# A fused attention and expert layer: sharing the first pooling, splitting stage 1 in 256 and 320 columns, and five smaller moves

## The chip, the core and the metric

The kernel runs on one core of a Trainium2 chip. A core has five engines with a queue of instructions each: TensorE (PE, matmuls; its weight loads are shown as PEld), VectorE (DVE), ScalarE (ACT), GpSimd (POOL) and SyncE (SP, which only issues transfers here). They run side by side and wait for each other through semaphores. The metric is the device time of one execution in microseconds (us).

## What is computed

Attention over keys and values that are averaged in groups of eight, and then a layer of eight experts with a fixed capacity. Cut to what matters:

```python
# q, k, v: 8 batches, 8 heads, 576 positions, 64 per head
k_p, v_p = mean of k, v over groups of 8 positions      # 72 left
scores = q @ k_p^T / 8 ; attn = softmax(scores) ; x = attn @ v_p
x = x as 4608 tokens of 512
logits = x @ w_gate                                     # 4608 x 8
order = argsort(-logits.flatten())
for idx in order:                                       # greedy
    tok, e = idx // 8, idx % 8
    if tok is free and expert e has under 576 tokens: assign tok to e
out[mask_e] = relu(x[mask_e] @ w1[e]) @ w2[e]           # 512 -> 1024 -> 512
```

All is float32. The greedy assignment fills one expert after another; the kernel finds, expert by expert, the threshold at which an expert is full, and the experts are computed in the order in which they fill.

## The kernel before

**Attention.** The 4608 tokens are 36 tiles of 128; a batch is four and a half tiles. For tile n the loop records: `st_s(n)`, scores of q against the pooled keys `kblk` into the PSUM tile `pss` (one buffer, so the next scores wait until softmax has read it); `st_e(n-1)`, transposes of the exponentials; `st_av(n-2)`, the product with `vblk` into `psa`; `softmax(n)`, a maximum (L181) and a subtraction (L182) on DVE and the exponential (L183) on ACT; and `norm(n-3)` on DVE, after which ACT's queue stores tile x to DRAM (`xd`). One instruction stream per engine is recorded in that order, and each engine works its stream strictly in order.

Ahead of a batch its k is pooled by `pool_k` (sums of halves, L117, L118, L121, the last writes `kblk`) and its v by `pool_v` (L133 to L135 write the sums `vsum`; then `vblk` gets its blocks, L139 by six ACT activations for the first v or L142 as one masked product). `prep_v` and `prep_g` are the small transposes and gate products that complete `vblk` (L150 to L161). The first k and v are pooled by DVE, all later ones by POOL, at tiles that the table `at` names with `plan`. The loads are issued by SP in the order k, q, v; those of the first batch are cut into halves. `warm(n)` records n matmuls of ones by ones whose result nobody reads; 16 of them stand ahead of the first tile, six after each of tiles 0 and 1.

**Search.** `Routing` works on logits of 128 x 36 x 8. `bounds` finds their largest and smallest value, in three steps that `A.run` places after given norms of the attention's last third. Then, per expert, some rounds of comparing (DVE L520) and counting (PE L525) narrow the threshold. `close` turns the selection into a list of rows (`rows`, `halves`), counts which expert got how much (`per`, `pc`, then PE L671 `rt<-pc,ones` and DVE's `left`), checks the result (`bad`) and takes the chosen tokens out of the logits with two masks (L695, L696). It is a generator; each `yield` names how long the next piece needs, and a piece is called a step.

**Experts.** The rows of x are gathered by POOL (`xg`, five tiles of up to 128 rows), transposed by PE (L916) into `tp`, and split into a rounded part `xh` (ACT L918) and the rest `xl` (DVE L920). Weights are split likewise: `w1h` (ACT L892), `w1l` (DVE L896). Stage 1 (L936) makes h = xh·w1h + xh·w1l + xl·w1h, for two column halves of 288 tokens and eight groups of 128 hidden units each; ACT and DVE split the relu of it into `hh` and `hl`. Stage 2 (L963, 512 columns, four token tiles, and L974 for the remaining 64 tokens) multiplies with w2, ACT copies and POOL scatters rows to the output.

The order of all this is written by a planner in `experts`: `now` counts estimated PE time along the matmuls of stages 1 and 2, `dve` estimated DVE time, and pieces of the next expert's search, its weight splits (`Pieces`) and its transposes (`turn`) are recorded between matmuls when their estimated time has come; `later` holds back DVE work. For the first expert there is no stage before it, so its steps are written out one after the other.

**End.** After the experts `suspect` makes a flag from `bad` (PE L750, DVE L751). All engines load the flag (L1011), and a branch runs `experts_one_by_one` if it is set.

Of the kernel before, what the change touches and what calls it, by code (L numbers as in the profile page):

```python
# [21 lines left out]
class Attention:  # L22
# [100 lines left out]
    def pool_v(self, b, eng, halves=(slice(0, 6),), first=False):  # L123

        src = self.rv[b]
        t1 = self.wk.tile([96, 6, 256], F32, name="t1", bufs=1)
        t2 = self.wk.tile([96, 6, 128], F32, name="t2", bufs=1)
        if b not in self.sums:
            self.sums[b] = self.wk.tile([96, 6, 64], F32, name="vsum")
        s = self.sums[b]  # L130
        for c in halves:
            n = c.stop - c.start
            eng.tensor_tensor(t1[:, c], src[:, c, :256], src[:, c, 256:], op=OP.add)  # L133
            eng.tensor_tensor(t2[:, c], t1[:, c, :128], t1[:, c, 128:], op=OP.add)
            eng.tensor_tensor(s[:, c], t2[:, c, :64], t2[:, c, 64:], op=OP.add)  # L135
            if first:
                for m in range(c.start, c.stop):
                    for i in range(2):
                        self.nc.scalar.activation(self.vblk[b % 4][:96, m, i, :64], s[:, m], AF.Copy,  # L139
                                                  scale=self.mask[:, m, i:i + 1])  # L140
            else:
                eng.tensor_tensor(self.vblk[b % 4][:96, c, :, :64], s[:, c, None, :].to_broadcast([96, n, 2, 64]),  # L142
                                  self.mask[:, c, :, None].to_broadcast([96, n, 2, 64]), op=OP.mult)
# [94 lines left out]
    def finish(self, after):  # L238

        i, j = self.nt - 2, self.nt - 1  # L240
        rinv = {}
        self.st_e(j, 0)
        self.st_av(i, 0)
# [19 lines left out]
    def run(self, ctx, consts, after, end, warm):  # L263
# [22 lines left out]
        for b in (1, 2):  # L286
            self.load_k(b)
            self.load_v(b)
            self.load_q(b)
# [11 lines left out]
        for n in range(nt):  # L301
# [5 lines left out]
            if n == 2:  # L307
                self.prep_v(0)
                self.prep_g(0)
# [7 lines left out]
            if n < 2:  # L317
                self.pool_v(0, nc.vector, vh[n:n + 1], n == 0)
# [16 lines left out]
class Routing:  # L335
# [76 lines left out]
    def warm(self, n):  # L412


        ps = self.psum()
        for _ in range(n):
            self.nc.tensor.matmul(ps, self.ones, self.ones[:, None].to_broadcast([128, 4, 128]), start=True, stop=True)  # L417
# [327 lines left out]
    def suspect(self, flag):  # L745
        nc = self.nc
        b = self.wk.tile([128, 1], BF, name="rc")
# [3 lines left out]
        nc.vector.tensor_scalar(flag, ps[:1, :1], 0.0, None, op0=OP.is_gt)  # L751

# [86 lines left out]
class Experts:  # L839
# [82 lines left out]
    def stage1(self, later=lambda after, t, f: f()):  # L922
# [5 lines left out]
        for u in range(2):  # L928
            for f in range(8):
                o = slice(288 * u, 288 * u + 288)  # L930
                ps = self.psA.tile([128, 512], F32, name="h", bufs=5)
                n = 0
                for a, b in ((self.w1h, self.xh), (self.w1l, self.xh), (self.w1h, self.xl)):
                    for j in range(4):
                        fs = slice(128 * f, 128 * f + 128)
                        nc.tensor.matmul(ps[:, :288], a[:, j, fs], b[:, j, o], start=(n == 0), stop=(n == 11))  # L936
                        n += 1
                        if n < 12:
                            yield 0.133
                yield 0.133  # L940
                nc.scalar.activation(hh[:, f, o], ps[:, :288], AF.Relu)  # L941
                if u:
                    nc.scalar.activation(hr[:, f], ps[:, 224:288], AF.Relu)
                later(0.65, 0.4, lambda f=f, o=o, ps=ps: nc.vector.scalar_tensor_tensor(  # L944
                    hl[:, f, o], ps[:, :288], 0.0, hh[:, f, o].bitcast(F32), op0=OP.max, op1=OP.subtract))
# [39 lines left out]
def kernel(ctx, tc, q, k, v, wblk, moe_w1, moe_w2, out):  # L985
# [15 lines left out]
    with ExitStack() as c2:  # L1001
# [3 lines left out]
        A.run(c2, lambda: R.consts(A.jp, A.ident), {NC - 13: [step], NC - 12: [step], NC - 11: [step], NC - 5: [lambda: R.best(0, NC - 4)]},  # L1005
              R.begin(g), R.warm)
    with ExitStack() as c2:
        experts(c2, tc, g, R, xd, moe_w1, moe_w2, out, A.ident, cap)
    flag = cst.tile([1, 1], I32, name="flag")
    R.suspect(flag)  # L1010
    flag = nc.values_load(flag[0:1, 0:1], min_val=0, max_val=1)  # L1011
# [5 lines left out]
def experts(ctx, tc, g, R, xd, w1, w2, out, ident, cap):  # L1017

# [10 lines left out]
    now, dve, ready = 0.0, 0.0, 0.0  # L1029
# [12 lines left out]
    def step(e):  # L1042

        nonlocal now, ready, dve
# [17 lines left out]
        since[p, what] = now  # L1062

# [60 lines left out]
    eids = {}  # L1124
    while (0, "rows") not in since:
        step(0)

# [18 lines left out]
    last = 0.0  # L1146
    for e in range(8):
# [27 lines left out]
        if more:  # L1175
# [5 lines left out]
            for t in range(turned[e + 1], 3):  # L1181
                turn(e + 1, t)
        flush(2)
    flush()

# [74 lines left out]
```

## Time and profile before

| | us |
|---|---|
| median of 3 runs | 653.32 |
| lowest and highest | 651.98, 653.77 |
| profiled execution, its own time | 653.45 |
| its span | 651.7 |
| PE busy in the span | 610.7 (94%) |
| DVE busy | 399.7 (61%) |
| ACT busy | 241.3 (37%) |
| POOL busy | 187.5 (29%) |
| mean granted PE clock | 0.967 of full speed |

The span is measured from the first instruction to the last; 1.75 us of the profiled execution lie around it. The stages follow each other in time: attention to about 151, search and the way into the first expert to about 187, experts to 637, then the end. A row of the timeline has the start, the duration, the engine, the line, what is written and read, and in brackets how long the engine had been idle and what ended that. The row of a window has the busy time and the number of instructions of each engine. Busy time of PE includes time in which a matmul runs at half the clock.

### The profile page before, as it was taken

How to read it: one execution, taken by the hardware profiler on the slowest of the kernel's cores; microseconds unless marked ns; L12 is line 12 of the kernel's file. 1: busy time of each engine (PE TensorE's matmuls, PEld its weight loads, DVE VectorE, ACT ScalarE, POOL GpSimd, SP SyncE). 2: the span in 40 equal slices, each digit the busy share in tenths (PEclk: the TensorE clock that was granted, in tenths of full speed). 3: DMA queues.
4: the chain of work that ended last, by engine and by line, in shares of the span. 5: the costliest groups of instructions: out<-in, count | busy, mean ns of one | idle time of the engine just before them, and what ended most of it. 6: DMA issues, size and time to landing. Idle time of an engine off the chain costs nothing.

```text
span 651.7 us, 12033 instructions
## 1 busy us (share of the span) xinstructions
PE 610.7 (94%) x4638; PEld 528.2 (81%) x4638; DVE 399.7 (61%) x1137; ACT 241.3 (37%) x550; POOL 187.5 (29%) x203
## 2 busy tenths in 40 slices
PE   6899999996689999999999999999999999999990
PEld 3799999885389769877987997898799889879970
DVE  8677777878668577857874686387458327406200
ACT  3344444442335134514433353243336325415210
POOL 5899999000300330313301301130120112020010
PEclk9799999997779999999999999999999999999996
DMA  9999994111450524504501910460181055013011
GB/s 306 300 361 320 336 335 177 65 66 66 138 194 2 188 93 139 189 33 160 213 17 39 319 32 34 154 219 10 41 310 46 32 180 193 16 57 131 1 48 30
DMA packets 32291, 91.10 MB, mean 140 GB/s; under 512 B 3456, under 2 KB 3456, under 8 KB 29760
## 3 DMA queue, kind: packets, MB, share of 16 engines
q1 hardware_dynamic: 21008, 61.87, 27.8%
q0 software_dynamic: 5888, 18.88, 8.4%
q10 hardware_dynamic: 5328, 9.49, 4.3%
q8 instruction: 38, 0.62, 0.4%
q14 instruction: 29, 0.24, 0.1%
HBM read 71.35 MB, written 18.87 MB: 138 GB/s over the span
## 4 chain that ended last, share of the span: by engine, by line
PE 73%; issue 13%; DVE 8%; POOL 2%; ACT 1%; POOLq 0%; DVEq 0%; ACTq 0%
PE h L936 26%; PE h L963 20%; PE psa L206 8%; PE pss L171 5%; PE h L974 3%; PE tp L916 2%; PE pse L196 2%; PE rt L196 2%; POOL out_dram L950 1%; PE rt L645 1%; PE rt L562 1%; DVE e L182 1%; POOL xg L884 1%; PE rt L417 1%; PE rt L160 1%
## 5 line engine op out<-in xcount | busy, mean ns | idle before, releaser
L950 POOL DMA_INDIRECT out_dram<-yt,rows x32 | 33.9, 1061 | 289.8 <-ACT yt L967 289.5
L963 PE MATMUL h<-w2l,hh 128*128 128x512 f32 x256 | 102.2, 399 | 0.0
L963 PE MATMUL h<-w2h,hl 128*128 128x512 f32 x256 | 102.1, 399 | 0.0
L963 PE MATMUL h<-w2h,hh 128*128 128x512 f32 x256 | 101.2, 395 | 0.0
L936 PE MATMUL h<-xl,w1h 128*128 128x288 f32 x512 | 93.3, 300 | 3.6 <-DVE xl L920 3.6
L936 PE MATMUL h<-xh,w1l 128*128 128x288 f32 x512 | 95.2, 301 | 0.4 <-DVE late L1131 0.2
L936 PE MATMUL h<-xh,w1h 128*128 128x288 f32 x512 | 92.7, 300 | 0.7 <-ACT xh L918 0.7
L941 ACT ACTIVATE hh<-h 128x288 fp32r<-128x288 f32 x128 | 52.7, 412 | 100.7 <-PE h L936 95.6
L936 PEld LDWEIGHTS h<-xl,w1h 128*128 128x128 f32 x512 | 76.6, 189 | 3.8 <-DVE xl L920 3.8
L936 PEld LDWEIGHTS h<-xh,w1h 128*128 128x128 f32 x512 | 75.7, 189 | 4.3 <-issue 2.7
L936 PEld LDWEIGHTS h<-xh,w1l 128*128 128x128 f32 x512 | 76.6, 189 | 1.8 <-DVE w1l L896 0.8
L944 DVE SCALAR_TENSOR_TENSOR hl<-h,hh 128x288 fp32r<-128x288 f32 x128 | 57.5, 452 | 32.9 <-ACT hh L941 19.6
L206 PE MATMUL psa<-vblk,eT 97*128 97x146 f32 (+1 forms) x480 | 67.9, 294 | 0.5 <-DVE vblk L161 0.4
L884 POOL DMA_INDIRECT xg<-xd,rows x40 | 39.5, 988 | 94.5 <-DVE rows L656 60.4
L967 ACT ACTIVATE yt<-h 128x512 f32<-128x512 f32 x32 | 19.1, 598 | 122.7 <-PE h L963 106.2
L206 PEld LDWEIGHTS psa<-vblk,eT 97*128 97x128 f32 (+1 forms) x480 | 58.3, 183 | 2.5 <-issue 2.0
L963 PEld LDWEIGHTS h<-w2h,hl 128*128 128x128 f32 x256 | 48.2, 188 | 8.6
L963 PEld LDWEIGHTS h<-w2h,hh 128*128 128x128 f32 x256 | 48.2, 188 | 8.6
L963 PEld LDWEIGHTS h<-w2l,hh 128*128 128x128 f32 x256 | 48.3, 189 | 8.3
L171 PE MATMUL pss<-kblk,rawq 128*128 128x144 f32 (+1 forms) x320 | 44.1, 296 | 3.3 <-POOL eT L80 1.6
L896 DVE TENSOR_TENSOR w1l<-raw,w1h 128x512 fp32r<-128x512 f32 x64 | 41.0, 684 | 9.7 <-ACT w1h L892 9.5
L905 DVE TENSOR_TENSOR w2l<-raw,w2h 128x512 fp32r<-128x512 f32 x64 | 43.3, 683 | 0.5
(195 smaller groups left out, 907.8 us busy)
## 6 DMA issues: line engine op xcount, KB each, us to landing
raw<-in_moe_w_dram SPq DMA_DIRECT2D x64, 512.0 KB, 5.9
xd<-xt ACTq DMA_DIRECT2D x36, 256.0 KB, 6.3
rawk<-in_k_dram SPq DMA_DIRECT2D x7, 1152.0 KB, 13.5
rawv<-in_v_dram SPq DMA_DIRECT2D x7, 1152.0 KB, 16.5
rawq<-in_q_dram SPq DMA_DIRECT2D x7, 1152.0 KB, 12.1
rawk<-in_k_dram SPq DMA_DIRECT2D x2, 576.0 KB, 4.0
rawv<-in_v_dram SPq DMA_DIRECT2D x2, 576.0 KB, 9.7
rawq<-in_q_dram SPq DMA_DIRECT2D x1, 640.0 KB, 10.7
```

The source lines that it names most:

```text
L171: nc.tensor.matmul(ps[cols, j // 2, 144 * (j % 2):144 * (j % 2) + 144], self.q_of(b, j, n, cols.stop - cols.start), self.kblk[b % 4][:, j] ...
L196: nc.tensor.transpose(ps[:96, 128 * m:128 * m + 128], self.e[i][:, 96 * c:96 * c + 96], self.ident)
L206: self.nc.tensor.matmul(o[h], self.eT[i][:, g, 128 * m + h.start:128 * m + h.stop], self.vblk[b % 4][:, 3 * g + m], start=(m == 0), stop=( ...
L884: nc.gpsimd.indirect_dma_start(out=self.xg[:n, t, :], out_offset=None, in_=self.xd, in_offset=bass.IndirectOffsetOnAxis(ap=rows[:n, t:t + ...
L896: self.nc.vector.tensor_tensor(l, raw, h.bitcast(F32), op=OP.subtract)
L905: self.nc.vector.tensor_tensor(self.w2l[:, i], self.raw2[e][:, i], self.w2h[:, i].bitcast(F32), op=OP.subtract)
L936: nc.tensor.matmul(ps[:, :288], a[:, j, fs], b[:, j, o], start=(n == 0), stop=(n == 11))
L941: nc.scalar.activation(hh[:, f, o], ps[:, :288], AF.Relu)
L944: later(0.65, 0.4, lambda f=f, o=o, ps=ps: nc.vector.scalar_tensor_tensor(hl[:, f, o], ps[:, :288], 0.0, hh[:, f, o].bitcast(F32), op0=OP. ...
L950: st = nc.gpsimd.indirect_dma_start(out=rows, out_offset=bass.IndirectOffsetOnAxis(ap=idx, axis=0), in_=y, in_offset=None)
L963: nc.tensor.matmul(ps, a[:, f, o], b[:, f], start=(f == 0 and k == 0), stop=(f == 7 and k == 2))
L974: nc.tensor.matmul(ps[64 * a:64 * a + 64, :256], self.hr[:, f], self.raw2[e][:, f, 256 * a:256 * a + 256], start=(f == 0), stop=(f == 7))
```

## The change

- The first half of the first v is pooled by POOL, the second half by DVE, which now comes after the second tile's softmax. The buffers t1 and t2 are made once per batch, so both halves share them.
- The second k is pooled by DVE instead of POOL, in two halves, after the softmax of tile 2. Of the second q the part that the first tiles need is loaded ahead of the second v, the rest behind it. Four more idle matmuls stand ahead of `prep_v(0)`.
- The order of the last `st_e` and `st_av` in `finish` is swapped in one place.
- The three steps of `bounds` come two tiles later.
- In the search of the first expert three idle matmuls follow a step of the search that is announced with 1.25 or 2.2, and eight one with 2.6. They write to a tile `h` of the experts' PSUM.
- For the first expert the counts of `pc` come ahead of the ten idle matmuls, the first four weight splits ahead of `left` and the checks, and two tiles instead of three are transposed before stage 1 begins.
- Stage 1 goes over columns 0 to 255 and then 256 to 575, instead of two halves of 288; before stage 1 of every later expert two tiles are turned.
- The flag is made at the 24th matmul of the last stage 2 and loaded at the 48th.

```diff
+        self.pool_v(0, nc.gpsimd, vh[:1], True)
         for b in range(1, B):
-            plan(first[b - 2] + 1 if b > 2 else b, self.pool_k, b, nc.gpsimd)
+            if b == 1:
+                plan(2, self.pool_k, b, nc.vector, kh)
+            else:
+                plan(first[b - 2] + 1 if b > 2 else b, self.pool_k, b, nc.gpsimd)
...
+        n = 4 * self.cut(1)
+        self.load_k(1)
+        self.load_q(1, slice(0, n))
+        self.load_v(1)
+        self.load_q(1, slice(n, 4 * S))
...
             if n == 2:
+                warm(4)
                 self.prep_v(0)
...
-            if n < 2:
-                self.pool_v(0, nc.vector, vh[n:n + 1], n == 0)
+            if n == 1:
+                self.pool_v(0, nc.vector, vh[1:])
...
         i, j = self.nt - 2, self.nt - 1
-        self.st_e(j, 0)
         self.st_av(i, 0)
+        self.st_e(j, 0)
...
-        for u in range(2):
+        for o in (slice(0, 256), slice(256, 576)):
+            m = o.stop - o.start
+            dt = m / 2400 + 0.017
             for f in range(8):
...
-        A.run(c2, ..., {NC - 13: [step], NC - 12: [step], NC - 11: [step], NC - 5: [...]},
+        A.run(c2, ..., {NC - 11: [step], NC - 10: [step], NC - 9: [step], NC - 5: [...]},
...
+    def warm(n):
+        R.warm(n, psB.tile([128, 512], F32, name="h", bufs=5))
     while (0, "rows") not in since:
         step(0)
+        n = {1.25: 3, 2.2: 3, 2.6: 8}.get(gap, 0)
+        if n:
+            warm(n)
...
-    R.warm(10)
+    step(0)
     w1 = pieces[0] = Pieces(0, X.high1, X.low1)
-    for _ in range(4):
-        step(0)
     for i in range(4):
         w1.next(i < 3)
     X.load_1(behind(0), 2, 4)
+    step(0)
+    warm(10)
     since[0, "rows"] = -20.0
-    now = dve = -2.0
-    for t in range(3):
-        turn(0, t, *(("tp", 2), ("tp", 2), ("h", 5))[t])
+    now = dve = -1.0
+    for t in range(2):
+        turn(0, t)
+    flush()
...
+            if not more and n == 24:
+                assert next(g, None) is None
+                flag = R.suspect()
+            elif not more and n == 48:
+                flag = nc.values_load(flag[0:1, 0:1], min_val=0, max_val=1)
```

What this does to the order is seen at three places. The first is DVE from the first tile's subtraction on. `t` and `vsum` belong to the pooling of v, `tk` and `kblk` to that of k, `mx` and `e` to the softmax. Before:

```order
L182 TENSOR_TENSOR e<-pss,mx 128x576
L133 TENSOR_TENSOR t_248<-rawv 96x768
L134 TENSOR_TENSOR t_249<-t_248 96x384
L135 TENSOR_TENSOR vsum<-t_249 96x192
L181 TENSOR_REDUCE mx<-pss 128x8
L182 TENSOR_TENSOR e<-pss,mx 128x576
L133 TENSOR_TENSOR t_287<-rawv 96x768
L134 TENSOR_TENSOR t_288<-t_287 96x384
L135 TENSOR_TENSOR vsum<-t_288 96x192
L142 TENSOR_TENSOR vblk_203<-vsum,mask 96x6x64
L161 TENSOR_TENSOR vblk_203<-rt,mask 96x12x8
L181 TENSOR_REDUCE mx<-pss 128x8
```

The same engine of the changed kernel, from the gate product of the first v to the softmax of tile 3 (lines have moved by one):

```order
L162 TENSOR_TENSOR vblk_204<-rt,mask 96x12x8
L182 TENSOR_REDUCE mx<-pss 128x8
L183 TENSOR_TENSOR e<-pss,mx 128x576
L117 TENSOR_TENSOR tk_348<-rawk 128x576
L118 TENSOR_TENSOR tk_349<-tk_348 128x288
L121 TENSOR_TENSOR kblk_130<-tk_349 64x2x72 x2
L117 TENSOR_TENSOR tk_348<-rawk 128x576
L118 TENSOR_TENSOR tk_349<-tk_348 128x288
L121 TENSOR_TENSOR kblk_130<-tk_349 64x2x72 x2
L182 TENSOR_REDUCE mx<-pss 128x8
L183 TENSOR_TENSOR e<-pss,mx 128x576
```

Three operations on v have left DVE ahead of the second softmax, and eight on k stand between the softmax of tile 2 and that of tile 3.

The second place is POOL after its first settings. In the changed kernel:

```order
L134 TENSOR_TENSOR t_233<-rawv 96x768
L135 TENSOR_TENSOR t_234<-t_233 96x384
L136 TENSOR_TENSOR vsum<-t_234 96x192
L134 TENSOR_TENSOR t_293<-rawv 96x1536
L135 TENSOR_TENSOR t_294<-t_293 96x768
L136 TENSOR_TENSOR vsum<-t_294 96x384
L143 TENSOR_TENSOR vblk_205<-vsum,mask 96x12x64
L117 TENSOR_TENSOR tk_358<-rawk 128x1152
```

The half of the first v is new at the top, and the second k, which stood there in three rows, is gone; the second v and the third k follow as before.

The third place is DVE behind the first expert's rows. Before, and behind it the changed kernel:

```order
L668 TENSOR_REDUCE pc<-per 128x8
L673 TENSOR_TENSOR left<-need,rt 128x8
...
L695 TENSOR_TENSOR lg<-lg,pen_2135 128x288
L696 TENSOR_TENSOR lg<-lg,pen_2137 128x288
L502 TENSOR_SCALAR width<-hi,lo_186 128x1
L504 TENSOR_SCALAR steps<-shares,width 128x4
L506 RECIPROCAL scale<-steps 128x1
L896 TENSOR_TENSOR w1l<-raw_2025,w1h 128x512 x4
L1131 COPY late<-eid 1x1
L920 TENSOR_TENSOR xl<-tp,xh 128x4x128
```

```order
L678 TENSOR_REDUCE pc<-per 128x8
L908 TENSOR_TENSOR w1l<-raw_2045,w1h 128x512 x4
L1148 COPY late<-eid 1x1
L683 TENSOR_TENSOR left<-need,rt 128x8
...
L703 TENSOR_SCALAR pen_2181<-pick 128x8
L932 TENSOR_TENSOR xl<-tp,xh 128x4x128 x2
L705 TENSOR_TENSOR lg<-lg,pen_2179 128x288
L706 TENSOR_TENSOR lg<-lg,pen_2181 128x288
```

The four weight splits have moved ahead of the counts' difference and the checks, and the two masks have moved behind the first two differences of x.

More of the change, by code (lines that the diff above doesn't have):

```diff
@@ L1004 @@
         step = lambda: next(bounds, None)
-        A.run(c2, lambda: R.consts(A.jp, A.ident), {NC - 13: [step], NC - 12: [step], NC - 11: [step], NC - 5: [lambda: R.best(0, NC - 4)]},
+        A.run(c2, lambda: R.consts(A.jp, A.ident), {NC - 11: [step], NC - 10: [step], NC - 9: [step], NC - 5: [lambda: R.best(0, NC - 4)]},
               R.begin(g), R.warm)
     with ExitStack() as c2:
[L1008 to L1011, printed above, removed]
+        flag = experts(c2, tc, g, R, xd, moe_w1, moe_w2, out, A.ident, cap)
     with tc.If(flag > 0):
@@ L1027, in experts @@
     held, waiting = [], []
-    now, dve, ready = 0.0, 0.0, 0.0
+    now, dve, ready, gap = 0.0, 0.0, 0.0, 0.0
     def later(after, t, f):
@@ L1042, in step @@
     def step(e):
-        nonlocal now, ready, dve
+        nonlocal now, ready, dve, gap
         p, crit, t, what = held.pop() if held else next(g, (None, 0.0, 0.0, None))
@@ L1062, in step @@
         since[p, what] = now
+        gap = crit
         now += 0.2
@@ L1180, in experts @@
                 w1.next()
-            for t in range(turned[e + 1], 3):
+            for t in range(turned[e + 1], 2):
                 turn(e + 1, t)
@@ L1184, in experts @@
     flush()
+    return flag
 def experts_one_by_one(ctx, tc, R, xd, w1, w2, out, ident, cap):
```

39 lines of the change are left out of this document (20 added, 19 removed).

## Prediction

> **What bounds the kernel now.** I read the table of windows first, because the mean over the program hides three stages with different limits. Its columns are: window, length, busy time and instructions of PE, PEld, DVE, ACT and POOL, then the granted clock, DMA share and GB/s.
>
> ```profile
> 22.20:29.00 6.80, 6.53 (x28) 6.44 (x29) 2.22 (x4) 1.09 (x3) 6.55 (x4) 0.50 1.06 373
> 151.00:167.00 16.00, 7.61 (x179) 6.26 (x177) 12.39 (x60) 2.93 (x11) 0.42 (x1) 0.64 0.22 68
> 176.00:187.00 11.00, 6.96 (x32) 5.76 (x30) 8.77 (x23) 3.61 (x8) 0.00 (x0) 0.69 0.30 96
> 211.00:637.00 426.00, 424.92 (x3064) 363.02 (x3060) 239.63 (x720) 154.55 (x364) 79.26 (x113) 1.00 0.32 111
> ```
>
> From 211 to 637 us PE is busy 424.92 of 426.00 us at full clock: nothing the change does to another engine can shorten these 426 us, only fewer or shorter matmuls could. What is left to gain lies at four seams: the start (half clock from 22.20 to 29.00), the last attention tiles, the stretch from search to first expert (151 to 187, clock 0.64 and 0.69 in the two rows), and the tail.
>
> **Stage 1 in columns of 256 and 320.** The chain of waits gives runs of matmuls without a gap: stage 2 with 512 columns, stage 1 with 288.
>
> ```profile
> 344.49 11.21 PE h L963 x49
> 371.27 9.92 PE h L936 x74
> ```
>
> That is 229 ns and 134 ns a matmul, so 95 ns for 224 columns, or 0.424 ns a column. A 256 column matmul is then estimated at 120.4 ns, one of 320 at 147.6, together 268.0, which is twice 134.0. Cost: nothing. It is hidden by nothing either; it simply sums to the same. A fixed cost per matmul that the two rows do not separate could shift this by some 0.2 us an expert. What the split does bring is at the first expert: 256 columns are two token tiles, so its first matmul needs two transposed tiles instead of three.
>
> **The start.** Here the change moves most. The timeline of before (start, duration, engine, line):
>
> ```profile
> 1.77 1.60 POOL L68 MEMSET kblk<- 128x576 f32 x3
> 1.88 1.52 DVE L65 TENSOR_SCALAR mask<-row 96x3 f32<-96x3 int32 x1
> 4.76 0.33 SPq L93 DMA_DIRECT2D rawv<-in_v_dram  x1
> 8.66 0.76 DVE L117 TENSOR_TENSOR tk<-rawk 128x576 f32<-128x576 f32 x1
> 9.45 0.46 DVE L118 TENSOR_TENSOR tk<-tk 128x288 f32<-128x288 f32 x1
> 9.95 0.62 DVE L121 TENSOR_TENSOR kblk<-tk 64x144 f32<-64x144 f32 x2
> 14.45 0.35 DVE L135 TENSOR_TENSOR vsum<-t 96x192 f32<-96x192 f32 x1
> 14.84 1.55 ACT L139 ACTIVATE vblk<-vsum,mask 96x64 f32<-96x64 f32 x6 [1.16 <-DVE vsum L135]
> 17.42 2.76 POOL L117 TENSOR_TENSOR tk<-rawk 128x1152 f32<-128x1152 f32 x1 [8.10 <-DMA rawk<-in_k_dram]
> 17.75 2.65 DVE L135 TENSOR_TENSOR vsum<-t 96x192 f32<-96x192 f32 x1
> 20.26 1.40 POOL L118 TENSOR_TENSOR tk<-tk 128x576 f32<-128x576 f32 x1
> 20.43 1.65 DVE L142 TENSOR_TENSOR vblk<-vsum,mask 96x384 f32<-96x384 f32 x1
> 23.02 0.76 DVE L182 TENSOR_TENSOR e<-pss,mx 128x576 f32<-128x576 f32 x1
> 23.66 3.42 POOL L133 TENSOR_TENSOR t<-rawv 96x1536 f32<-96x1536 f32 x1
> 27.16 1.80 POOL L134 TENSOR_TENSOR t<-t 96x768 f32<-96x768 f32 x1
> 28.33 0.76 DVE L181 TENSOR_REDUCE mx<-pss 128x8 f32<-128x576 f32 x1 [4.54 <-PE pss L171]
> 29.04 1.00 POOL L135 TENSOR_TENSOR vsum<-t 96x384 f32<-96x384 f32 x1
> 30.12 1.47 POOL L142 TENSOR_TENSOR vblk<-vsum,mask 96x768 f32<-96x768 f32 x1
> ```
>
> The same L135 on the same shape takes 0.35 us at 14.45 and 2.65 at 17.75, where it begins inside POOL's L117 and ends 0.2 after it. L142 begins as L118 has begun and again ends after it. So a VectorE operation on operands in SBUF stands still while a GpSimd one runs, and between two dependent VectorE operations GpSimd's next one is let in. The three memsets at 1.77, which wait for nothing in between, passed as one group before L65 was served. [...]
>
> The change takes 2.30 us of waiting from L135 (2.65 less 0.35), because POOL no longer pools the second k at 17.42, but puts the six vblk activations (1.55) ahead of the first exponential. Softmax of tile 2, which ended at 23.78 (L182), should end at about 22.5; the two ends of this are 22.0 and 23.6. Then VectorE meets eight new operations ahead of the softmax of tile 3: twice L117, L118 and L121 x2, 0.76 + 0.46 + 0.62 = 1.84, so 3.7 us undisturbed, on the path. The extra transfer that splits q costs SP one more issue of 0.33, in front of transfers that wait for landings anyway: 0. Beside the eight lies GpSimd's chain for the second v. Its landing is read from the DMA view:
>
> ```profile
> rawv<-in_v_dram SPq DMA_DIRECT2D x3, 1152.0 KB, 17.1
> ```
>
> 4.76 + 17.1 = 21.9, and now 640 KB of q go first, at 373 GB/s 1.7 us more: 23.6. By then VectorE has done L117 and L118 (22.5 + 1.22 = 23.7). I let each engine pass its group that has no wait inside: POOL 3.42 to 27.1, VectorE L121 x2 and L117 (1.38) to 28.5, POOL 1.80 to 30.3, L118 to 30.8, POOL 1.00 to 31.8, L121 x2 to 32.4. The softmax of tile 3 starts at 32.4 instead of 28.33: 4.1 us late. Late next are the scores of tile 4, which need pss free, and PE, idle for most of 25 to 32, falls to half clock as it did at 22.20; I add 0.4 for that (0 to 2). **Start: +4.5 us.** Lower bound: no operation meets another, softmax 2 at 22.5 and the clock kept by the added warm matmuls, tile 3 at 22.5 + 3.7 = 26.2, less 0.9 for matmuls that were at half clock: -3.1. Upper bound: rival two. GpSimd's own part of the first v (from 10.1) can meet L121 of the first k: 0 to 1.0, I take 0, since it ends before softmax 0 is done.
>
> **Bounds of the search, two tiles later.** Their three steps put PE and VectorE work into tiles that also carry the preparation of a v. Nine tiles are one period; the softmax starts around the same three intervals, a period earlier and here:
>
> ```profile
> 77.83 0.76 DVE L181 TENSOR_REDUCE mx<-pss 128x8 f32<-128x576 f32 x1 [0.54 <-PE pss L171]
> 88.35 0.76 DVE L181 TENSOR_REDUCE mx<-pss 128x8 f32<-128x576 f32 x1 [0.81 <-PE pss L171]
> 109.19 0.76 DVE L181 TENSOR_REDUCE mx<-pss 128x8 f32<-128x576 f32 x1 [0.55 <-PE pss L171]
> 121.97 0.76 DVE L181 TENSOR_REDUCE mx<-pss 128x8 f32<-128x576 f32 x1 [0.53 <-PE pss L171]
> ```
>
> 12.78 against 10.52: the steps cost 2.26. One of the three may still meet such a tile; I keep 0.65 of it. **-1.6 us** (0 to -2.3). The swap of one st_e and st_av in the finish moves PE work that VectorE's row of softmax and norm covers: 0; without that cover one run of transposes would show, well under 1 us.
>
> **Search.** Four steps of it get three idle matmuls each, and a later one eight.
>
> ```profile
> 151.76 1.75 ACT L260 ACTIVATE xt<-psa,rinv 128x64 f32<-128x64 f32 x8 [0.48 <-DVE oh L474]
> 153.57 1.36 PE L525 MATMUL rt<-oh,cmp 128*32 128x8 bf16 x36 [0.88 <-DVE cmp L520]
> 166.62 4.42 PE L417 MATMUL rt<-ones 128*128 128x512 bf16 x10 [0.32 <-DVE halves L660]
> ```
>
> At half clock one costs 0.44 (4.42 over 10), at full half of it. Three are 0.66 in a gap of 0.88, which hides them; at half clock they are 1.33 and stick out by 0.45 a round. The first three also wait for the PSUM tile behind the activations that end at 153.51, which holds L525 back by about 0.65. **+0.65 to +1.45; I take +1.0.** A higher clock alone shortens little here: VectorE is busy 12.39 of the 16.00 us from 151 to 167, PE 7.61.
>
> **First expert.** The rows in order:
>
> ```profile
> 166.97 0.66 DVE L668 TENSOR_REDUCE pc<-per 128x8 bf16<-128x288 bf16 x1
> 172.61 1.16 ACT L918 ACTIVATE xh<-tp 128x512 fp32r<-128x512 f32 x2 [2.46 <-PE tp L916]
> 175.22 0.80 PE L936 MATMUL h<-xh,w1h 128*128 128x288 f32 x4 [0.69 <-ACT xh L918]
> 181.38 1.09 PE L936 MATMUL h<-xl,w1h 128*128 128x288 f32 x3 [3.62 <-DVE xl L920]
> 210.93 0.48 PE L963 MATMUL h<-w2h,hh 128*128 128x512 f32 x1
> 301.85 0.79 PE L936 MATMUL h<-xh,w1h 128*128 128x288 f32 x4
> 330.64 0.39 PE L963 MATMUL h<-w2h,hh 128*128 128x512 f32 x1
> ```
>
> pc is ready at 167.63, but L671 (the count of pc) stands behind ten idle matmuls until 166.62 + 4.42 = 171.04; the masks that follow it delay w1l and xl, for which PE waits 3.62. Now L671 goes first, w1l follows pc, and the masks come after the first two xl. PE can begin when two tiles are transposed, at the end of the xh pair, 173.8. An undisturbed stage 1 takes 28.8 (330.64 less 301.85), so stage 2 could begin at 202.6 instead of 210.93: 8.3 earlier. Two waits come in: transposes that stand in PE's queue behind the third xl (about 1), and the eighth w1l, now behind masks and best on VectorE (about 1.3): 6.0. If both vanish 8.3, if half clock stays as it is in 176 to 187 about 4.5. **-6.0, with the search -5.0 net** (-3.5 to -7.4). [...]
>
> **Tail.** The flag's load on GpSimd is the one on the chain:
>
> ```profile
> 637.24 0.50 POOLq L1011
> ```
>
> It now stands in the last stage 2, under PE's work: **-0.45** (0 to -0.5).
>
> **Sum.** The profiled execution took 653.45, 0.13 above the median of 653.32. 653.45 + 4.5 - 1.6 - 5.0 - 0.45 = **650.9 us**.
>
> **Rivals.** One: no collision at the start (-3.1 instead of +4.5): 643.3. For it: VectorE needs only 3.7 us, and if v lands later than 25 most are through. Against it: 17.75. Two, the slower side: engines alternate one for one on the shared operands, and between L118 and the last L121 GpSimd's pooling of the third k, which waits only for that L118, gets in. 23.7 + 3.42 + 0.31 + 1.80 + 0.31 + 1.00 + 0.76 + 1.47 + 0.46 + 2.76 (the same shape as at 17.42) + 0.62 = 36.6, 8.3 late, plus 0.4, and half clock for 3.4 us more, half of what it lasted from 22.20, which costs half of that, 1.7: start +10.4, total 656.8. It decides slower once the start loses over 8.9. For it: L142 let POOL in although it followed L135 by 0.03; against it: the memsets' group. Three: alternation without that k: 33.9, 5.5 late, start +5.9, total 652.3, no change. Four: first expert at its lower bound (-3.5) with the forecast's start: 652.4 too.
>
> **Chances.** Forecast 0.42 (its own range 649.4 to 651.9), rival one 0.14, two 0.18, three 0.16, four 0.10. A difference below 0.3% (1.96 us, so 651.4 to 655.3) cannot be told from no change here. Faster: rival one and three quarters of the forecast, 0.46. Slower: rival two and a little of three, 0.20. Same: 0.34. The range reaches into both far cases: 643.5 to 657.0.
>
> **What would show it.** In the changed profile: L117, L118 and L121 on VectorE near 23 to 33 with durations of 2 to 4 us, the reduce of tile 3 at about 32, half clock up to 36 or 39; no 3.62 at the first xl and the first L963 some 5 us closer to the end of attention. I am wrong if these VectorE rows keep 0.76 and 0.46, or if the first stage 2 does not come closer.

## The result and the profile after

The changed kernel takes 659.03 us (median of 9 runs, 654.14 to 662.17), the kernel before 651.17 us (9 runs, 648.29 to 654.48). The ratio is 1.0105 with a 95% interval of 1.0071 to 1.0140: it became slower by about 1%, where I forecast 0.4% faster, and it lies outside my range of 643.5 to 657.0. Here and below, medians are of all runs, but ratios compare fast runs alone: a run over 1.5% above the fastest of its kernel is left out, three of ten for the kernel with the second k one tile earlier and at most one in any other experiment.

The profiled execution took 659.56 us, 6.1 more than that of before. A ledger of the two traces, from one event to the next (softmax starts are those of L181 before and L182 after, "rows" is DVE's cast of the first expert's rows, "stage 1" and "stage 2" the first matmul of each for the first expert):

| stretch | before | after | difference | forecast |
|---|---|---|---|---|
| start to softmax of tile 5 | 35.76 | 45.58 | +9.82 | +4.5 |
| tile 5 to tile 35 | 108.07 | 106.44 | -1.63 | -1.6 |
| tile 35 to rows | 22.50 | 26.60 | +4.10 | +1.0 |
| rows to stage 1 | 8.88 | 7.61 | -1.27 | -1.4 |
| stage 1 of the first expert | 35.72 | 33.01 | -2.71 | -4.6 |
| to the last matmul of stage 2 of the last expert | 425.46 | 425.31 | -0.15 | 0 |
| from there to the end of the span | 15.27 | 13.21 | -2.06 | -0.45 |

The differences sum to 6.1, where the forecast's sum to -2.55. The start alone is more than all of it. Here is its timeline in the changed kernel, DVE and POOL only (start, duration, engine, line):

```profile
10.25 1.97 POOL L134 TENSOR_TENSOR t<-rawv 96x768 f32<-96x768 f32 x1 [0.93 <-DMA rawv<-in_v_dram]
10.59 1.89 DVE L77 TENSOR_SCALAR vblk<-mask 96x12 f32<-96x12 f32 x4
...
18.37 0.35 DVE L136 TENSOR_TENSOR vsum<-t 96x192 f32<-96x192 f32 x1
18.75 0.55 DVE L143 TENSOR_TENSOR vblk<-vsum,mask 96x384 f32<-96x384 f32 x1
...
22.61 0.76 DVE L183 TENSOR_TENSOR e<-pss,mx 128x576 f32<-128x576 f32 x1
23.29 0.75 DVE L117 TENSOR_TENSOR tk<-rawk 128x576 f32<-128x576 f32 x1
24.00 3.42 POOL L134 TENSOR_TENSOR t<-rawv 96x1536 f32<-96x1536 f32 x1 [10.01 <-DMA rawv<-in_v_dram]
24.07 3.67 DVE L118 TENSOR_TENSOR tk<-tk 128x288 f32<-128x288 f32 x1
27.50 1.91 POOL L135 TENSOR_TENSOR t<-t 96x768 f32<-96x768 f32 x1
27.86 2.79 DVE L121 TENSOR_TENSOR kblk<-tk 64x144 f32<-64x144 f32 x2
29.49 0.99 POOL L136 TENSOR_TENSOR vsum<-t 96x384 f32<-96x384 f32 x1
30.55 1.47 POOL L143 TENSOR_TENSOR vblk<-vsum,mask 96x768 f32<-96x768 f32 x1
30.66 1.98 DVE L117 TENSOR_TENSOR tk<-rawk 128x576 f32<-128x576 f32 x1
32.67 0.46 DVE L118 TENSOR_TENSOR tk<-tk 128x288 f32<-128x288 f32 x1
33.17 2.94 DVE L121 TENSOR_TENSOR kblk<-tk 64x144 f32<-64x144 f32 x2
33.21 2.73 POOL L117 TENSOR_TENSOR tk<-rawk 128x1152 f32<-128x1152 f32 x1 [1.19 <-DVE tk L118]
36.13 0.76 DVE L182 TENSOR_REDUCE mx<-pss 128x8 f32<-128x576 f32 x1
```

Two things are to be seen. VectorE is now free of the 2.30 us of waiting in the first v (L136 takes 0.35), as intended. And its eight operations on the second k, 3.7 us of work, take from 23.29 to 36.11: while POOL is busy, one of them gets through behind each POOL operation, and the one after it waits until the next POOL operation is done. Even the two L121, which follow each other without a wait, let L136 of POOL in (27.86, lasting until 30.65), and at the end POOL's L117 on the third k, released by DVE's L118, goes ahead of the last L121. This is the order of my second rival, one for one, and the softmax of tile 3 starts at 36.13 where that rival had 36.6. It begins one operation earlier than there, at L118: the softmax of tile 2 ends at 23.37 (22.61 + 0.76), not at 22.5. On top, POOL's part of the first v, in the first row above, stands in the way of four small L77, which take 1.89 us. In the kernel before they take 0.40:

```profile
10.60 0.40 DVE L77 TENSOR_SCALAR vblk<-mask 96x12 f32<-96x12 f32 x4
```

I had bounded what this part of the first v can meet at 1.0 and taken it as nothing.

PE finds nothing to do meanwhile. The windows of the changed kernel (busy time and instructions of PE, PEld, DVE, ACT, POOL, then clock, DMA share, GB/s):

```profile
29.03:32.44 3.41, 0.00 (x0) 0.00 (x0) 3.38 (x3) 0.00 (x0) 2.83 (x3) 1.00 0.99 236
32.44:35.86 3.42, 0.00 (x0) 0.00 (x0) 3.34 (x4) 0.00 (x0) 2.65 (x1) 0.57 0.96 372
35.86:39.27 3.41, 0.95 (x8) 0.98 (x10) 2.69 (x6) 0.68 (x1) 2.96 (x4) 0.50 1.10 365
39.27:42.68 3.41, 3.41 (x21) 2.97 (x19) 1.99 (x5) 0.49 (x1) 3.33 (x2) 0.50 0.92 216
42.68:46.10 3.42, 3.42 (x28) 3.23 (x27) 0.98 (x2) 1.60 (x4) 3.19 (x4) 0.93 0.40 148
```

Here the clock falls from 1.00 to 0.50 at 32.95 us, behind 3.41 us without a matmul (29.54 to 32.95), and comes back to 1.00 at 43.19, behind 3.41 us in which PE is busy for 3.41 (39.78 to 43.19), so tile 4 and the beginning of tile 5 run at half clock too.

### The profile page after: what moved, and what is told of

It reads as the page before. It is cut to its first block, busy times and chain, and to the rows that moved or that the text cites. A ratio compares the mean times of both kernels' runs of the same rounds, so it can differ in the third digit from the quotient of the medians.

```text
span 657.8 us, 12083 instructions
## 1 busy us (share of the span) xinstructions
PE 618.4 (94%) x4662; PEld 533.1 (81%) x4662; DVE 408.2 (62%) x1142; ACT 242.7 (37%) x550; POOL 187.1 (28%) x202
## 4 chain that ended last, share of the span: by engine, by line
PE 71%; issue 15%; DVE 6%; POOL 3%; DMA 2%; ACT 1%; POOLq 0%; SPq 0%; DVEq 0%; ACTq 0%
PE h L949 25%; PE h L976 19%; PE psa L207 8%; PE pss L172 5%; PE h L987 3%; PE tp L928 2%; PE pse L197 2%; DMA xg<-xd,rows 2%; PE rt L197 2%; POOL out_dram L963 2%; POOL xg L896 1%; DVE kblk L121 1%; PE rt L572 1%; PE rt L655 1%; DVE tk L118 1%
## 5 line engine op out<-in xcount | busy, mean ns | idle before, releaser
L949 PE MATMUL h<-xl,w1h 128*128 128x320 f32 (+1 forms) x512 | 95.3, 302 | 0.0
L949 PE MATMUL h<-xh,w1h 128*128 128x320 f32 (+1 forms) x512 | 92.1, 301 | 0.7 <-ACT xh L930 0.7
L949 PE MATMUL h<-xh,w1l 128*128 128x320 f32 (+1 forms) x512 | 92.7, 300 | 0.0
L954 ACT ACTIVATE hh<-h 128x320 fp32r<-128x320 f32 (+1 forms) x128 | 51.9, 410 | 101.0 <-PE h L949 100.6
L957 DVE SCALAR_TENSOR_TENSOR hl<-h,hh 128x320 fp32r<-128x320 f32 (+1 forms) x128 | 57.3, 451 | 28.4 <-ACT hr L956 18.4
L932 DVE TENSOR_TENSOR xl<-tp,xh 128x512 fp32r<-128x512 f32 (+1 forms) x40 | 25.3, 633 | 78.9 <-ACT xh L930 78.8
L172 PEld LDWEIGHTS pss<-kblk,rawq 128*128 128x128 f32 (+1 forms) x320 | 38.5, 186 | 15.9 <-issue 14.2
```

Source lines behind the costliest of these rows:

```text
L172: nc.tensor.matmul(ps[cols, j // 2, 144 * (j % 2):144 * (j % 2) + 144], self.q_of(b, j, n, cols.stop - cols.start), self.kblk[b % 4][:, j] ...
L932: later(1.3, 0.65, lambda: nc.vector.tensor_tensor(xl, ps[:, :, :n], xh, op=OP.subtract))
L949: nc.tensor.matmul(ps[:, :m], a[:, j, fs], b[:, j, o], start=(n == 0), stop=(n == 11))
L954: nc.scalar.activation(hh[:, f, o], ps[:, :m], AF.Relu)
L957: later(0.65, 0.4, lambda f=f, o=o, m=m, ps=ps: nc.vector.scalar_tensor_tensor(hl[:, f, o], ps[:, :m], 0.0, hh[:, f, o].bitcast(F32), op0= ...
```

## Experiments

The theory after the comparison: **collision**, the start's loss comes from the second k on VectorE beside GpSimd's sums. Its rivals: VectorE has too much work in the start wherever it stands, or the loss comes from sharing the first v and the later second v. For the stretch from search to first expert: the idle products are in the way, or they keep the clock for the first expert. All ratios are to the kernel before on the same chip.

### The second k on GpSimd again

```diff
-            if b == 1:
-                plan(2, self.pool_k, b, nc.vector, kh)
-            else:
-                plan(first[b - 2] + 1 if b > 2 else b, self.pool_k, b, nc.gpsimd)
+            plan(first[b - 2] + 1 if b > 2 else b, self.pool_k, b, nc.gpsimd)
```

> The changed kernel with the second k pooled by POOL again, all else as changed. Theory 'collision' (the start's loss of 9.8 us comes from the eight operations on k on VectorE standing against GpSimd's sums): the reduce of tile 3 starts at 26 to 29 instead of 36.13, tile 5 at 35 to 37 instead of 45.58, and the kernel is 8.5 to 10 us faster than the changed one, so 2 to 4 us faster than before. Rival 'share' (the loss comes from the first v being shared and the second v landing 2 us later): tile 5 stays at 40 or later, and the kernel is at most 5 us faster than the changed one.

Measured: 650.1 us, ratio 0.9941 (0.9913 to 0.9970). Tile 3 starts at 25.93 instead of 36.13:

```profile
25.93 0.76 DVE L182 TENSOR_REDUCE mx<-pss 128x8 f32<-128x576 f32 x1 [1.71 <-PE pss L172]
```

Tile 5 starts at 33.66, earlier than the 35 to 37 I expected and 2.1 us earlier than before; in this profile the clock stays full through the whole start (its mean over the program is 0.979, before 0.967), and the old start alone spreads by more than that from profile to profile (last section), so no gain is shown by it. With this one edit put back, 1.0105 becomes 0.9941, some 10.7 us. The rival "share" is out.

### The second k on VectorE, but one tile earlier

```diff
-                plan(2, self.pool_k, b, nc.vector, kh)
+                plan(1, self.pool_k, b, nc.vector, kh)
```

> The changed kernel with the eight operations on the second k on VectorE one tile earlier, ahead of the second v's landing, where GpSimd has nothing to do. Theory 'collision': L117, L118 and L121 keep 0.76, 0.46 and 0.62 us, the reduce of tile 2 comes 1 to 2 us later than 21.84, that of tile 3 at 26 to 28, and the kernel is 9 to 11 us faster than the changed one, 2 to 5 faster than before. Rival 'work' (VectorE has 3.7 us too many in the start, wherever they stand): tile 3 at 30 or later, 5 us faster than the changed one at most.

Measured: 648.64 us, ratio 0.9918 (0.9890 to 0.9947). The timeline of this kernel:

```profile
19.27 0.75 DVE L117 TENSOR_TENSOR tk<-rawk 128x576 f32<-128x576 f32 x1
20.05 0.46 DVE L118 TENSOR_TENSOR tk<-tk 128x288 f32<-128x288 f32 x1
20.62 0.62 DVE L121 TENSOR_TENSOR kblk<-tk 64x144 f32<-64x144 f32 x2
21.25 0.76 DVE L117 TENSOR_TENSOR tk<-rawk 128x576 f32<-128x576 f32 x1
22.05 0.46 DVE L118 TENSOR_TENSOR tk<-tk 128x288 f32<-128x288 f32 x1
22.54 0.62 DVE L121 TENSOR_TENSOR kblk<-tk 64x144 f32<-64x144 f32 x2
23.37 0.74 DVE L182 TENSOR_REDUCE mx<-pss 128x8 f32<-128x576 f32 x1
23.48 3.43 POOL L134 TENSOR_TENSOR t<-rawv 96x1536 f32<-96x1536 f32 x1 [9.46 <-DVE vblk L162]
...
29.39 0.76 DVE L182 TENSOR_REDUCE mx<-pss 128x8 f32<-128x576 f32 x1 [4.49 <-PE pss L172]
```

The same eight operations on the same engine take 3.9 us instead of 12.8, because POOL has nothing to do until 23.48. So it is not the amount of work on VectorE but what it lies beside. The kernel is some 12 us faster than the changed one (1.0105 against 0.9918), where the rival "work" allowed 5. Tile 3 starts at 29.39, later than the 26 to 28 I expected: it waits 4.49 us for PE, so the k is not what holds it.

### The kernel before with that one edit alone

```diff
-            plan(first[b - 2] + 1 if b > 2 else b, self.pool_k, b, nc.gpsimd)
+            if b == 1:
+                plan(2, self.pool_k, b, nc.vector, kh)
+            else:
+                plan(first[b - 2] + 1 if b > 2 else b, self.pool_k, b, nc.gpsimd)
```

> The kernel before with one edit: the second k is pooled by VectorE in two halves behind the softmax of tile 2. Theory 'collision': L118 and L121 stretch to 2 to 4 us beside GpSimd's sums of the second v, the reduce of tile 3 at 33 to 37 instead of 28.33, 6 to 10 us slower than before. Rival 'it needs the rest of the start too' (v sharing, later second v): under 4 us slower.

Measured: 660.68 us, ratio 1.0097 (1.0071 to 1.0123). Tile 3 starts at 34.26. From its timeline:

```profile
21.93 3.63 POOL L133 TENSOR_TENSOR t<-rawv 96x1536 f32<-96x1536 f32 x1 [12.61 <-DMA rawv<-in_v_dram]
22.30 3.58 DVE L118 TENSOR_TENSOR tk<-tk 128x288 f32<-128x288 f32 x1
25.63 1.90 POOL L134 TENSOR_TENSOR t<-t 96x768 f32<-96x768 f32 x1
25.98 2.79 DVE L121 TENSOR_TENSOR kblk<-tk 64x144 f32<-64x144 f32 x2
...
34.26 0.76 DVE L181 TENSOR_REDUCE mx<-pss 128x8 f32<-128x576 f32 x1
```

One edit alone makes the kernel as slow as the whole change. The collision needs neither the shared v nor the later transfer; taken away (two runs above) the loss goes, put in alone it comes. Its size depends on what stands around it: 0.97% here, some 6.3 us, against the 10.7 us that taking it out of the changed kernel brought. Why the two differ was not tried.

### The whole start as before

```diff
-        self.pool_v(0, nc.gpsimd, vh[:1], True)
-                warm(4)
-            if n == 1:
-                self.pool_v(0, nc.vector, vh[1:])
+            if n < 2:
+                self.pool_v(0, nc.vector, vh[n:n + 1], n == 0)
... (and the loads and the second k as before)
```

> The changed kernel with the whole start as before: both halves of the first v on VectorE, second k on POOL, second q whole behind the second v, no four idle matmuls. Everything else as changed. If the rest of the change is worth what the stages of the last profiles say (bounds -1.65, search +2.5 to +3.7, way into the first expert and its stage 1 -5.5, end -1 to -2), tile 5 starts at 35.8 as before and the kernel is 5 to 6 us faster than before. Rival 'the rest is worth nothing, the gain over the changed kernel is all in the start': within 2 us of before.

Measured: 647.88 us, ratio 0.9908 (0.9884 to 0.9932), 6.0 us faster than before. Tile 5 starts at 34.23. By time the rest of the change is worth what its stages were expected to give, and this is the lowest ratio of all runs. Against it the kernel with the second k on POOL and the first v shared has 0.9941; the intervals overlap, so whether sharing the first v costs anything is not settled, but it brought nothing that could be measured.

### The idle products of the search

```diff
-        n = {1.25: 3, 2.2: 3, 2.6: 8}.get(gap, 0)
-        if n:
-            warm(n)
```

> The changed kernel without the idle products in the search (three after a round, eight after a later step). Theory 'in the way' (they hold back the counts and do not keep the clock): from the last softmax to the rows 2 us less, first expert as before, the kernel 1.5 to 2.5 us faster than the changed one. Rival 'they keep the clock for the first expert': the search gets 2 us shorter, but the first expert's stage 1 meets more half clock and takes 2 us more, no difference.

> The changed kernel with the second k on POOL and without the idle products of the search. Theory 'in the way': 2 to 3 us faster than with the products (650.1 there against 652.99 of before, ratio 0.994), so a ratio of about 0.990. Rival 'they keep the clock': ratio 0.994 to 0.996, with a longer stage 1 of the first expert (over 32 us instead of 31.3).

> The changed kernel with the second k on VectorE one tile earlier and without the idle products of the search. As the one with k on POOL: theory 'in the way' 2 to 3 us faster than with the products (ratio 0.992 there), so about 0.988; rival 'they keep the clock' 0.992 or more.

> The changed kernel with the start as before and without the idle products of the search. With them the ratio was 0.9908 (0.9884 to 0.9932). Theory 'what the search gains stage 1 loses': from the last softmax to the rows 2 to 3.7 us less, first stage 1 1 to 4 us more, ratio 0.989 to 0.992. Theory 'in the way': 0.987 or less.

| base | with them | without | search, with | without | first stage 1, with | without |
|---|---|---|---|---|---|---|
| changed kernel | 1.0105 (1.0071-1.0140) | 1.0096 (1.0060-1.0132) | 16.07 | 14.04 | 33.01 | 32.83 |
| second k on POOL | 0.9941 (0.9913-0.9970) | 0.9918 (0.9889-0.9948) | 16.31 | 14.02 | 31.29 | 35.03 |
| second k earlier | 0.9918 (0.9890-0.9947) | 0.9927 (0.9896-0.9957) | 16.31 | 14.02 | 31.44 | 32.62 |
| start as before | 0.9908 (0.9884-0.9932) | 0.9941 (0.9900-0.9982) | 16.07 | 14.03 | 30.77 | 32.53 |

"Search" is from the first `g<-rt,need` to the rows; before it took 14.02. Without the products the search is 2.0 to 2.3 us shorter, as the theory "in the way" has it, but in three of the four pairs the first stage 1 is 1.2 to 3.7 us longer. That is about the rival's size, but only in the pair with the second k on POOL is it the rival's reason: there the half clock inside this stage 1 grows from 0 to 6.8 us. In the other two it lasts as long with the products as without (none, and 3.3 and 3.4 us), and PE's waits inside the stage are longer instead (2.56 us with the products and 2.75 + 0.45 without; 0.27 and 2.18). The four differences of the ratios, -0.0009, -0.0023, +0.0009 and +0.0033, have both signs and lie inside their intervals: no difference. The profile of the changed kernel shows that the products do not bring the clock back during the rounds:

```profile
165.56:168.98 3.42, 3.17 (x58) 2.08 (x56) 2.19 (x10) 0.00 (x0) 0.00 (x0) 0.50 0.02 5
168.98:172.39 3.41, 2.99 (x47) 1.90 (x46) 1.90 (x10) 0.00 (x0) 0.00 (x0) 0.50 0.00 0
172.39:175.80 3.41, 3.13 (x10) 1.17 (x10) 2.87 (x18) 0.06 (x1) 0.00 (x0) 0.50 0.00 0
175.80:179.22 3.42, 2.49 (x49) 1.48 (x48) 2.00 (x7) 0.83 (x1) 0.00 (x0) 0.93 0.69 188
```

With three wide products (512 columns) and 36 small matmuls (8 columns) in a round PE is 3.17 and 2.99 us busy, and the clock stays at a half (0.50); it comes back (0.93 in the last row) behind the window that holds almost only wide ones. The clock itself changes at 162.66 and 176.31, half a microsecond beside borders of these rows; in the four stretches of 3.41 us between the two PE is busy 2.75, 2.93, 3.09 and 3.27 us. Busy time alone does not tell the two cases apart: the kernel with the start as before keeps half clock behind a window with 3.17 us (155.74 to 159.15), and the kernel before gets full clock behind one with 3.10 (168.98 to 172.39), which holds ten matmuls, wide products and transposes of 128 columns, and only one small one among them.

A variant keeps only the eight:

```diff
-        n = {1.25: 3, 2.2: 3, 2.6: 8}.get(gap, 0)
+        n = {2.6: 8}.get(gap, 0)
```

> The changed kernel with the start as before and only the eight idle products behind the last long step of the search, none behind its rounds. If the three behind each round only hold back the counts and the later ones keep the clock for the first expert, it has both gains: search 2 us less than 26.6, first stage 1 near 31, ratio 0.987 or less. If the clock needs them all: ratio 0.990 to 0.992 with a stage 1 of 32 to 35.

Measured: ratio 0.9921 (0.9884 to 0.9958), search 14.79, first stage 1 31.75. Its profile has both gains in part, the ratio does not tell it from its neighbours: inconclusive.

### The second half of the first w1 released later

```diff
-    X.load_1(behind(0), 2, 4)
     step(0)
     warm(10)
...
     flush()
+    X.load_1(behind(0), 2, 4)
```

> The changed kernel with the load of the second half of the first w1 (released by the copy 'late') behind the first two xl, where it comes after nearly all gathers have been issued. Theory 'transfers collide': the wait of PE's transposes for gathered rows (2.65 us) falls under 1, stage 1 of the first expert takes 1.5 to 2.5 us less than 33.0, the kernel is that much faster than the changed one. Rival 'the weights are then late': the wait for rows goes, but stage 1 waits as long for w1h of the second half; no difference or slower.

Measured: 662.23 us, ratio 1.0126 (1.0082 to 1.0169), first stage 1 35.77 instead of 33.01. In the changed kernel PE waits for the fourth gathered tile, and the copy that releases the rest of w1 now runs ahead of the last gather's issue:

```profile
182.79 0.13 DVE L1148 COPY late<-eid 1x1 int32<-1x1 int32 x1
185.27 0.90 POOL L896 DMA_INDIRECT xg<-xd,rows  x1 [0.30 <-issue]
191.73 0.63 PE L928 MATMUL tp<-ident,xg 128*128 128x128 f32 x4 [2.65 <-DMA xg<-xd,rows]
```

With the later release that wait is gone and a longer one is there:

```profile
187.14 0.13 DVE L1148 COPY late<-eid 1x1 int32<-1x1 int32 x1
192.08 1.15 ACT L904 ACTIVATE w1h<-raw 128x512 fp32r<-128x512 f32 x2 [5.58 <-DMA raw<-in_moe_w_dram]
195.26 0.69 PE L928 MATMUL tp<-ident,xg 64*128 64x64 f32 x4 [4.61 <-DVE xl L932]
```

VectorE waits 4.6 us for the late weights with w1l, and the xl behind it in its stream, which PE needs, waits with it. Each theory came half true: without the weights beside them the rows come in time, and with the weights behind, stage 1 is 2.76 us longer in the profile. By time the two kernels cannot be told apart (1.0126 against 1.0105), and the gain of 1.5 to 2.5 us did not come. The order of copy and gathers alone does not make the wait: the kernel with the start as before has the same order and waits 0.27 us at this place. What makes the rows late in the one and not in the other was not tried.

### Two halves of 288 columns

```diff
-        for o in (slice(0, 256), slice(256, 576)):
+        for o in (slice(0, 288), slice(288, 576)):
...
-    for t in range(2):
-        turn(0, t)
+    for t in range(3):
+        turn(0, t, *(("tp", 2), ("tp", 2), ("h", 5))[t])
```

> The changed kernel with the second k on POOL, and stage 1 again in two halves of 288 columns, three tiles turned ahead of it. Theory 'columns cost nothing and bring an earlier first matmul': first matmul of stage 1 about 1.3 us later after the rows (9.0 instead of 7.7), later experts' stage 1 the same within 0.3 us, so 1 to 1.5 us slower than with 256 and 320 (ratio 0.996 against 0.994). Rival 'the wait for the fourth tile takes it back anyway': stage 2 of the first expert begins equally late after the rows, no difference.

Measured: ratio 0.9957 (0.9929 to 0.9986) against 0.9941. From rows to stage 1 it takes 10.43 instead of 7.68 us, 2.75 more where I expected 1.3, and stage 1 then 30.08 instead of 31.29: together 1.5 us later in the profile, the upper end of the expected 1 to 1.5; by time the two cannot be told apart.

### The flag read at the end

```diff
-            if not more and n == 24:
-                assert next(g, None) is None
-                flag = R.suspect()
-            elif not more and n == 48:
-                flag = nc.values_load(flag[0:1, 0:1], min_val=0, max_val=1)
+    flag = R.suspect()
+    flag = nc.values_load(flag[0:1, 0:1], min_val=0, max_val=1)
```

> The changed kernel with the start as before and the flag made and read behind the experts as before. With the read in the last stage 2 the ratio was 0.9908. My predicted size of this edit is 0.45 us (ratio 0.9915), the profiles say 0.3 to 2.1 (0.991 to 0.994); the time from the last matmul to the end of the span should be 15.2 again instead of 13.2 to 14.9.

Measured: ratio 0.9936 (0.9901 to 0.9971) against 0.9908, intervals overlapping. From the last matmul of stage 2 to the end of the span the profiles have 15.27, 15.26 and 14.91 us with the flag at the end, and 13.21 to 14.94 (11 profiles) with the read inside stage 2. The two kernels that differ in this edit alone have 14.91 and 14.94: between their profiles there is no gain. Over all profiles it lies between nothing and 2.1 us, and time does not resolve it.

## Why the prediction was wrong

**The start: the term that failed.** The prediction let "each engine pass its group that has no wait inside", and so had VectorE through at 32.4 and +4.5 us for the start. The changed kernel shows one operation each in turn, groups or not, the third k's L117 ahead of the last L121, and 36.13. I had the durations of the operations right, and nearly the price of this order, in rival two (36.6, start +10.4, total 656.8), and gave it 0.18. Its start is 0.6 us off the measured +9.82; its total is 2.8 us under the 659.56 of the profiled execution, since it carries the forecast's other terms. What misled me were the three memsets at 1.77, from which I read that operations without a wait between them pass together. They are not what stands here: two L121 in a row did let POOL in (2.79 us instead of 0.62). The row that spoke for alternation, L142 beginning 0.03 after L135 and losing its place, was the same two engines with the same kind of operands, and should have decided. By time, the start is worth the difference between 1.0105 and 0.9908, 2.0% or about 13 us, where the two profiles give +9.8. A part of the difference is the spread of the starts: five profiles with the old start reach tile 5 at 32.03 to 35.76, of which that of the kernel before is the latest, and three with the new one at 44.54 to 45.73, on average 11.2 us apart.

**Half clock.** I gave it 0.4; the way from tile 3 to tile 5 took 4.42 + 5.03 = 9.45 against 3.75 + 3.68 = 7.43 before, 2.0 more; the granted clock was 0.50 from 32.95 to 43.19. Rival two had 2.1 in all.

**First v on POOL meeting other work:** bounded at 1.0, taken as 0, measured 0.99 at the softmax of tile 0 (12.40 against 11.41). The bound held, the choice was wrong, and what that part met was not what I had named: the L121 of the first k keep their 0.62, but the L77 behind them, which stand ahead of that softmax and which I overlooked, wait. How much of this reaches tile 3 is not shown; the softmax of tile 2 starts at 21.84, 0.4 earlier than before.

**Bounds:** -1.6 forecast, -1.63 measured, and -1.6 to -1.7 between tiles 26 and 35 in all profiles that have it. Right.

**Search:** +0.65 to +1.45 forecast, the products cost 2.0 (14.04 to 16.07). The clock was half through all rounds (0.50 from 162.66 to 176.31). The first round became 1.04 us longer, the next two 0.35 and 0.37, and the stretch from there to the rows 0.29. My own prices, 0.65 for the first wait and 0.45 a round at half clock, give 2.0 for three such rounds; my range ended at 1.45, so the sum was wrong and not the prices. The further 2.1 of the 4.10 in the ledger lie ahead of the first `g<-rt,need`, where a half clock fell on the last attention tiles (0.50 from 155.83 to 159.24; the kernel with the second k on POOL has 0.4 there).

**First expert:** -6.0 forecast; -3.98 in the changed kernel, -5.6 to -6.1 in the profiles with the second k on POOL, with it earlier, and with the start as before. Two tiles do bring the first matmul forward (7.6 instead of 8.9 us from rows to stage 1), and the 3.62 wait is gone. What stage 1 then takes is close to a sum: my undisturbed 28.8, PE's longest wait inside it, and half of the time at half clock inside it. Before, 28.8 + 3.62 + 6.8 / 2 = 35.8 (measured 35.72); in the changed kernel 28.8 + 2.65 + 3.4 / 2 = 33.2 (33.01); with the second k on POOL 28.8 + 2.41 = 31.2 (31.29); with the start as before 28.8 + 0.27 + 3.3 / 2 = 30.7 (30.77). The forecast was 28.8 + 2.3 for two waits, without half clock. The waits have about that size, so the half clock (0.50) from 193.38 to 196.79 is most of the 2 us that are missing. Of the two waits that I expected, the one at the transposes is there, but it waits for gathered rows beside the w1 transfer, not for the third xl: the copy `late`, which releases that transfer, was moved ahead by an edit whose transfers I did not follow.

**Columns:** nothing, as forecast; the seven later experts took 425.31 instead of 425.46 us with the first one's stage 2. A fixed cost per matmul, which I had allowed 0.2 us an expert, could not have moved it: both splits have 192 matmuls an expert.

**Tail:** -0.45 forecast, -2.06 in the ledger, and between nothing and -2.1 over all profiles. I counted the flag's load on POOL only. The time from POOL's branch to its next instruction fell as well, from 4.16 to 2.67 us in the changed kernel and to 2.70 with the start as before; but from the last scatter's issue to the end it took 14.19 us before, 12.12 in the changed kernel and 13.85 with the start as before. The trace of the last of these shows what holds its end: behind its branch POOL waits until the last scatter has landed, 4.48 us after the issue, where the changed kernel's landed after 2.59. Why the scatter takes longer there is not shown.

**Sum.** The profiled execution lies 8.7 us above the forecast of 650.9. Of these the start makes 5.3 (9.82 instead of 4.5), the search 3.1, the first expert 2.0, and the tail takes back 1.6. The start's order of service is the step that turned a forecast gain into a loss; by itself it gives 656.2, still inside my range, and it took the search and the first expert to leave it. That the terms without the start, forecast as -7.05, came out as -6.0 by time in the kernel with the start as before (ratio 0.9908) is in part luck: in the changed kernel the same stretches gave -3.7.

## What to carry to other kernels

Before work is moved to VectorE because it looks idle, lay its operations beside what GpSimd will do in the same microseconds: with operands in SBUF, both went one for one here, and 3.7 us of VectorE work took 12.8 us on the path. The same work moved one tile earlier, to where GpSimd had nothing to do, was part of a kernel 0.8% faster than before. And if one of two orders of service cannot be excluded and their prices lie 6 us apart, the row with the same engines and operands weighs more than one with other operations.

## What the runs showed of the hardware that I had not expected

- GpSimd was let in between two VectorE operations even where these followed each other without a wait (L121 x2 of the changed kernel: 2.79 us at 27.86 and 2.94 at 33.17 instead of 0.62).
- Four tiny VectorE operations with one SBUF operand (96 x 12) took 1.89 instead of 0.40 us beside a GpSimd sum (the first of them ends at 12.26, the sum at 12.22).
- PE was busy for 3.17 of 3.41 us with small matmuls and three wide ones and kept half clock (start as before, 155.74 to 159.15); behind 3.10 us of wide ones and 128-column transposes it got full clock (kernel before, 168.98 to 172.39).
- A kernel's time varies by about a percent between runs here (648.29 to 654.48 for the kernel before), and so do its stages. Five profiles share the old start; they reach tile 5 at 35.76, 35.30, 34.23, 33.06 and 32.03, and the half clock ahead of it lasts 6.8, 6.8, 3.4, 3.4 and 0 us in this order. In the profiles of the kernels before and after, a stretch at half clock between the start and the end of the experts lasted 3.41 us or 2, 3, 4 or 5 times that (6.83, 17.07 and 6.83 before; 3.41, 10.24, 3.41, 13.65, 3.41 and 3.41 after); where it fell in the program differed. The order fits, but that this is the cause of the spread was not tried.
